# Attention and two matmuls on one core: twelve steps' leaky ReLU and the first batch's token sums in another form

## The chip, the core and the metric

The program runs on one core of a Trainium2 chip. The core has five engines with a queue of instructions each: PE (TensorE, matmuls; its weight loads are listed as PEld), DVE (VectorE), ACT (ScalarE), POOL (GpSimd) and SP, which here only issues DMAs. Each engine takes its instructions in order, and semaphores hold an instruction back until what it reads is written. SBUF is the working memory; PE writes to PSUM, in eight banks of 128x512 fp32.

The metric is the device time of one execution in microseconds. Before the change three runs took 1013.35 to 1014.5 us, with a median of 1014.16.

## The reference: what is computed

Two parts in a row, all in fp32.

Attention, for 8 batches, 8 heads, 576 tokens of 64 values:

```python
q_d = q.reshape(B, H, Sd, 4, D).mean(axis=3)          # the same for k, v
out_d = softmax(q_d k_d^T / 8) v_d
out_up = np.repeat(out_d, 4, axis=2)
mask = np.abs(pos[:, None] - pos[None, :]) < 4
out_local = softmax(where(mask, q k^T / 8, -1e9)) v
x = (out_up + out_local) as 4608 tokens x 512
```

So each token attends to its neighbours at a distance below four, and the means of four tokens attend to one another ("down").

Then two matmuls with a leaky ReLU between them, whose slope alpha belongs to the column:

```python
h = x @ w_in                                           # 4608x512 by 512x2048
g = np.maximum(h, 0.0) + alpha * np.minimum(h, 0.0)
out = g @ w_out                                        # 4608x2048 by 2048x512
```

The inputs w_in and w_out come as 64-bit floats and are put into fp32 on the chip by integer operations on their halves ("decode").

## The kernel before

**The two matmuls, in steps.** The 4608 tokens make 18 chunks of 256, and the 2048 columns of w_in 8 blocks of 256, so there are 144 steps; step s works on chunk s // 8 and block s % 8. Every operand is split into a rounded high part and a low part, and three products are summed. In a step, hidden(s) (L743) writes h into a PSUM bank of the pair ph with 24 matmuls; slopes(s) (L756) reads it on ACT, for each half once with the scale slope into an SBUF tile t and once with the scale sign back into the same bank; larger(s) (L763) takes the maximum of the two on DVE; split(s) (L766) casts it to the high part gh on ACT and subtracts on POOL for the low part gl; product(s) (L786) adds 12 matmuls to the output banks. sign is +1 where alpha is at most 1 and -1 elsewhere, slope is sign times alpha, and w_out's rows carry sign, so the maximum is right for both.

**The order of the steps** is written out by hand. Every part enters a list with a due time, at(t, f, ...), counted in steps, and the list is worked off in order of these times (L915 to L917). hidden(s) stands at s - 1.95, slopes at s - 1.45, larger at s - 1.15, split at s - 1.0 and product at s + 0.6. So PE works in the order hidden(s), product(s-2), hidden(s+1), product(s-1), hidden(s+2), product(s).

**The attention of batches 1 to 7** stands in the same list: local (L566) for the neighbours, on DVE mostly, and down (L224) for the means, whose loads ld are folded four to one by POOL's adds (L72), turned and scored by PE (qkT L250, s L263, pT L287, pv L297) and copied between by ACT (kd L258, dp L273 and L282, th L291, od L302).

**The first batch** has its own code (L363 to L522) ahead of the list, and there the framework's scheduler sets the order on each engine, by its own estimate of times. Four pairs of heads pass through pair(hp): q and k are turned by PE into the banks f0T, f1T and copied by ACT to qb and kT; the windows' scores fs get a maximum fmx, a difference fp, an exponential, a sum fsm and a normalization (L481 to L488) on DVE and ACT; PE turns fp into fpT and weighs v into fpv; DVE adds the down part fod into fxs, and ACT and DVE split it into xh and xl (L512 to L519), the first chunks' operands. The sums of four tokens of q and k are taken from the loaded tiles by two adds each on DVE (L453, L455) and turned by PE (L460); those of v by two adds (L471, L473). The pairs' down part waits for them.

**The decode** of a block of weights (make, L161) runs magnitude on ACT (L184), reach (L188, L189) and bits (L193, L194) on DVE, upper on ACT (L199 for w_in, L203 for w_out) and lower on DVE (L207, L211). The ten blocks with fp below 5 run with the first batch, 128x1024 at a time with the temporary in SBUF; the last twelve half blocks stand in the list, 128x512 at a time with the temporary in PSUM. In the page's and the trace's names, woh and wol are the high and low part of w_out, wih and wil those of w_in.

## Time and profile before

| | |
|---|---|
| median of three runs | 1014.16 us |
| the profiled execution | 1012.62 us, its span 1010.8 us |
| PE busy | 960.6 us (95%), 6402 instructions |
| DVE busy | 832.8 us (82%), 1347 |
| ACT busy | 560.2 us (55%), 1483 |
| POOL busy | 482.1 us (48%), 612 |
| mean DMA rate | 97 GB/s over the span |

The page divides the span into 40 slices of 25.3 us and gives busy shares in tenths. PE is at 9 from the eighth slice on, DVE at 8 or 9 in nearly all slices but the last four, and the DMA engines at 8 and 9 in the first two. TensorE's granted clock is below 9 in four of the first five slices. A row of the groups gives a line, an engine, the operation, what it writes and reads, the shape, a count, the busy time and the mean in ns of one, and the engine's idle time just before. The view of waits gives the waiting instruction, the one that released it, the total, the count and the longest. Windows give busy times for stretches of the span.

### The profile page before, as it was taken

The page shows a single profiled execution, that of the slowest core. Times are in us where ns is not written, and L with a number is a line of the kernel's source. Part 1 is how long each engine was busy: PE and PEld are TensorE (multiplying, and loading weights), DVE is VectorE, ACT ScalarE, POOL GpSimd, SP SyncE. Part 2 cuts the span into 40 slices and gives each one's busy share as a digit, 9 for nine tenths or more (in the row PEclk, how much of TensorE's full clock was granted, in tenths as well). Part 3 has the DMA queues.
Part 4 walks back from the last instruction along what each step waited for, and adds up shares of the span by engine and source line. Part 5 has one row for each costly group of instructions (what it writes and reads, how often), then busy time and mean ns, then how long its engine had stood idle before and what let it go on. Part 6 is the DMA issues. An engine that isn't in the chain of part 4 may idle for free.

```text
span 1010.8 us, 17864 instructions
## 1 busy us (share of the span) xinstructions
PE 960.6 (95%) x6402; PEld 852.7 (84%) x6402; DVE 832.8 (82%) x1347; ACT 560.2 (55%) x1483; POOL 482.1 (48%) x612
## 2 busy tenths in 40 slices
PE   5877989999999999999999999999999999999998
PEld 4756878898888898988888888888988898989997
DVE  6899988899888899899888898898898899997111
ACT  4767766465565555555455555555555554444442
POOL 2040645677665546555554544656555543323221
PEclk9856989999999999999999999999999999999999
DMA  8946443232422322433322332322331412210000
GB/s 191 222 148 242 123 153 98 83 119 83 145 83 73 118 81 78 121 97 93 103 88 66 100 111 71 125 80 74 123 100 60 131 49 61 86 43 22 1 21 22
DMA packets 61218, 98.26 MB, mean 97 GB/s; under 512 B 21578, under 2 KB 26954, under 8 KB 61130
## 3 DMA queue, kind: packets, MB, share of 16 engines
q1 hardware_dynamic: 60938, 96.87, 32.0%
q8 instruction: 50, 0.82, 0.3%
q10 hardware_dynamic: 192, 0.26, 0.1%
q14 instruction: 38, 0.31, 0.1%
HBM read 87.67 MB, written 9.44 MB: 96 GB/s over the span
## 4 chain that ended last, share of the span: by engine, by line
PE 72%; DVE 15%; ACT 4%; issue 3%; DMA 2%; POOL 2%; SPq 2%; DVEq 0%; ACTq 0%; POOLq 0%
PE o L798 33%; PE h L752 33%; DMA raw<-in_moe_w_out 2%; DVE qk L591 2%; DVE lb L650 2%; PE s L263 2%; DVE t L764 1%; PE pv L297 1%; DVE ls L595 1%; DVE temp L193 1%; DVE pv L647 1%; PE xp L659 1%; PE pT L287 1%; DVE temp L194 1%; DMA ld<-in_q 1%
## 5 line engine op out<-in xcount | busy, mean ns | idle before, releaser
L69 POOL TENSOR_TENSOR gl<-t,gh 128x512 fp32r<-128x512 f32 x144 | 186.5, 1295 | 390.8 <-ACT gh L769 347.4
L760 ACT ACTIVATE t<-h,slope 128x256 f32<-128x256 f32 x288 | 136.3, 473 | 203.0 <-PE h L752 166.2
L764 DVE TENSOR_TENSOR t<-h,t 128x512 f32<-128x512 f32 x144 | 99.0, 687 | 113.2 <-ACT h L761 108.6
L752 PE MATMUL h<-xh,wih 128*128 128x256 f32 x1152 | 190.9, 287 | 0.7 <-ACT xh L518 0.7
L798 PE MATMUL o<-woh,gh 128*128 128x512 f32 x576 | 188.1, 407 | 0.4 <-ACT woh L203 0.4
L752 PE MATMUL h<-xl,wih 128*128 128x256 f32 x1152 | 183.7, 281 | 0.6 <-POOL xl L69 0.6
L752 PE MATMUL h<-xh,wil 128*128 128x256 f32 x1152 | 184.1, 282 | 0.0
L798 PE MATMUL o<-wol,gh 128*128 128x512 f32 x576 | 182.1, 397 | 0.1
L798 PE MATMUL o<-woh,gl 128*128 128x512 f32 x576 | 182.1, 397 | 0.0
L752 PEld LDWEIGHTS h<-xh,wih 128*128 128x128 f32 x1152 | 163.5, 190 | 10.5 <-issue 1.8
L72 POOL TENSOR_TENSOR ld<-ld 72x256 f32<-72x256 f32 x168 | 125.4, 747 | 73.9 <-DMA ld<-in_q 49.4
L752 PEld LDWEIGHTS h<-xl,wih 128*128 128x128 f32 x1152 | 156.9, 190 | 0.8 <-POOL xl L69 0.8
L752 PEld LDWEIGHTS h<-xh,wil 128*128 128x128 f32 x1152 | 157.3, 190 | 0.0
L769 ACT CAST gh<-t 128x512 fp32r<-128x512 f32 x144 | 89.1, 619 | 118.7 <-DVE t L764 68.4
L595 DVE TENSOR_REDUCE ls<-qk 128x12 f32<-128x768 f32 (+1 forms) x126 | 136.4, 1083 | 2.8
L798 PEld LDWEIGHTS o<-woh,gl 128*128 128x128 f32 x576 | 108.6, 189 | 26.4
L798 PEld LDWEIGHTS o<-wol,gh 128*128 128x128 f32 x576 | 108.4, 188 | 26.4 <-DVE wol L211 0.7
L761 ACT ACTIVATE h<-h,sign 128x256 f32<-128x256 f32 x288 | 126.4, 439 | 0.0
L650 DVE TENSOR_TENSOR lb<-lb,pv 128x384 f32<-128x384 f32 x202 | 113.9, 564 | 5.5
L798 PEld LDWEIGHTS o<-woh,gh 128*128 128x128 f32 x576 | 98.3, 189 | 16.3 <-issue 2.2
L647 DVE TENSOR_TENSOR pv<-v,lb 128x1152 f32<-128x1152 f32 x84 | 93.6, 1115 | 2.6
L591 DVE TENSOR_TENSOR qk<-k,qp 128x768 f32<-128x768 f32 (+1 forms) x78 | 84.0, 1077 | 0.0
(148 smaller groups left out, 1111.4 us busy)
## 6 DMA issues: line engine op xcount, KB each, us to landing
k<-in_k SPq DMA_DIRECT2D x41, 384.0 KB
v<-in_v SPq DMA_DIRECT2D x41, 384.0 KB
raw<-in_moe_w_in SPq DMA_DIRECT2D x16, 512.0 KB
raw<-in_moe_w_out SPq DMA_DIRECT2D x16, 512.0 KB
ld<-in_q SPq DMA_DIRECT2D x56, 144.0 KB
ld<-in_k SPq DMA_DIRECT2D x56, 144.0 KB
ld<-in_v SPq DMA_DIRECT2D x56, 144.0 KB
q<-in_q SPq DMA_DIRECT2D x42, 192.0 KB
```

The source lines that it names most:

```text
L69: nc.gpsimd.tensor_tensor(o, a, b, op=ALU.subtract)
L72: nc.gpsimd.tensor_tensor(o, a, b, op=ALU.add)
L591: nc.vector.tensor_tensor(st["pr"][:, :nd], window(tiles[u, "k"], half, d0, nd), st["qp", half].unsqueeze(1).to_broadcast([128, nd, 2, 192 ...
L595: nc.vector.tensor_reduce(out=st["s"][:, half, d0:d0 + nd, :].rearrange("p a b -> p (a b)"), in_=st["pr"][:, :nd].rearrange("p a h (t d) - ...
L647: nc.vector.tensor_tensor(st["pr"][:, :nd], window4(tiles[u, "v"], half, d0, nd), prob(half, d0, nd), op=ALU.mult)
L650: nc.vector.tensor_tensor(st["acc"], st["acc"], st["pr"][:, i], op=ALU.add)
L752: nc.tensor.matmul(ph[:, j], w[:, m, 128 * o:128 * o + 128], x[:, m, :], start=(i == 0), stop=(i == 11))
L760: nc.scalar.activation(t[:, j], hs[st][:, j], AF.Copy, scale=slope[:, f:f + 1])
L761: nc.scalar.activation(hs[st][:, j], hs[st][:, j], AF.Copy, scale=sign[:, f:f + 1])
L764: nc.vector.tensor_tensor(gs[st], hs.pop(st), gs[st], op=ALU.max)
L769: nc.scalar.copy(gh, t)
L798: nc.tensor.matmul(outs[c][m], g[:, j, 128 * m:128 * m + 128], wo[w][n][:, o, :], start=(f == 0 and i == 0), stop=(f == NF - 1 and i == 2))
```

## The change

It has three parts.

1. In steps 0 to 11 (EARLY = 12) the second activation of slopes no longer writes sign times h into the PSUM bank: it writes Relu(gain times h), with gain = sign - slope, into an SBUF tile of the pool late with the tag xf, which has one buffer; larger then adds the two on POOL, where before it took the maximum on DVE. The ph bank is free once ACT has read it. Steps 12 to 143 are as they were.
2. For the first batch's q and k, the sums of four tokens are reduced on DVE from the PSUM banks f0T and f1T after PE has turned the tokens. The adds ahead of the turn, the four transposes of the sums and the copy of k's sums are gone.
3. The first batch's two adds for v move from DVE to POOL.

```diff
+EARLY = 12
+    gain = const.tile([128, NF], F32, name="gain")
...
+        nc.vector.tensor_tensor(gain, sign, slope, op=ALU.subtract)
...
         def pair(hp):
+            sums = [st.tile([128, 144], F32, tag=f"fs{x}", name=f"fs{x}{hp}") for x in "qk"]
             for x in range(2):
                 for t0, nt in ((0, 4), (4, 4)):
...
+                    nc.vector.tensor_reduce(out=sums[x][:, 18 * t0:18 * t0 + 72], in_=ps.rearrange("p (t a) -> p a t", t=nt),
+                                            axis=AX.X, op=ALU.add)
...
-                    sums = []
-                    for i, x in enumerate("qk"):
-                        lv = qk[hp][:, i].rearrange("p (g f) h d -> p g (f h d)", g=2)
-                        s4 = lv[:, :, 0:256]
-                        nc.vector.tensor_tensor(s4, lv[:, :, 0:256], lv[:, :, 256:512], op=ALU.add)
-                        s2 = st.tile([72, 2, 128], F32, tag=f"fs2{x}", name=f"fs2{x}{hp}")
-                        nc.vector.tensor_tensor(s2, s4[:, :, 0:128], s4[:, :, 128:256], op=ALU.add)
-                        sums.append(s2)
-                    ps = ps_h.tile([128, 512], F32, tag="ph", name=f"fsum{hp}")
-                    for x in range(2):
-                        for g in range(2):
-                            nc.tensor.transpose(ps[:, (2 * x + g) * 72:(2 * x + g) * 72 + 72], sums[x][:, g],
-                                                ident[:72, :72])
...
-                    kd = st.tile([128, 144], F32, tag="fkh", name=f"fkd{hp}")
-                    nc.scalar.copy(kd, ps[:, 144:288])
...
-                        nc.tensor.matmul(sd[:, bl, :], qd[:, bl, :], kd, start=True, stop=True)
+                        nc.tensor.matmul(sd[:, bl, :], qd[:, bl, :], sums[1], start=True, stop=True)
...
-            nc.vector.tensor_tensor(lv[:, :, 0:128], lv[:, :, 0:128], lv[:, :, 128:256], op=ALU.add)
+            add(lv[:, :, 0:128], lv[:, :, 0:128], lv[:, :, 128:256])
...
-            nc.vector.tensor_tensor(vd.rearrange("p h g d -> p (h g) d"), lv[:, :, 0:64], lv[:, :, 64:128], op=ALU.add)
+            add(vd.rearrange("p h g d -> p (h g) d"), lv[:, :, 0:64], lv[:, :, 64:128])
...
     def slopes(st):
         t = gs[st] = two.tile([128, 2, T], F32, tag="t", name=f"t{st}")
+        other = hs[st]
+        if st < EARLY:
+            other = late.tile([128, 512], F32, tag="xf", name=f"sh{st}").rearrange("p (j n) -> p j n", j=2)
         for j in range(2):
             f = 2 * (st % NP) + j
             nc.scalar.activation(t[:, j], hs[st][:, j], AF.Copy, scale=slope[:, f:f + 1])
-            nc.scalar.activation(hs[st][:, j], hs[st][:, j], AF.Copy, scale=sign[:, f:f + 1])
+            if st < EARLY:
+                nc.scalar.activation(other[:, j], hs[st][:, j], AF.Relu, scale=gain[:, f:f + 1])
+            else:
+                nc.scalar.activation(other[:, j], hs[st][:, j], AF.Copy, scale=sign[:, f:f + 1])
+        if st < EARLY:
+            hs[st] = other

     def larger(st):
-        nc.vector.tensor_tensor(gs[st], hs.pop(st), gs[st], op=ALU.max)
+        if st < EARLY:
+            add(gs[st], hs.pop(st), gs[st])
+        else:
+            nc.vector.tensor_tensor(gs[st], hs.pop(st), gs[st], op=ALU.max)
```

Since the scheduler orders the first batch anew, more moves than the diff shows. In the rows below, a number after a name's first word tells the pair (fmx2, fp2), the half and block of weights (raw0_1 is w_in's block 1, raw1_3 w_out's block 3) or the step (t0, gl0); the last number only tells buffers apart.

DVE, around the start of the decode of w_out's block 1 (raw1_1, whose first DVE instruction is the tensor_scalar L188 behind raw0_1's last L194). Before:

```order
L482 TENSOR_TENSOR fp2_576<-fs20_532,fmx2_573 128x490
L189 TENSOR_SCALAR temp_791<-temp_791 128x1024
L453 TENSOR_TENSOR fqk3_157<-fqk3_157 72x2x256
L482 TENSOR_TENSOR fp2_576<-fs27_541,fmx2_573 128x140
L519 TENSOR_TENSOR xl1_328<-fxs04_325,xh1_327 128x256
L193 SCALAR_TENSOR_TENSOR temp_791<-raw0_1_167,temp_791 128x1024
L455 TENSOR_TENSOR fs2q3_679<-fqk3_157 72x256
L453 TENSOR_TENSOR fqk3_157<-fqk3_157 72x2x256
L194 SCALAR_TENSOR_TENSOR temp_791<-raw0_1_167,temp_791 128x1024
L188 TENSOR_SCALAR temp_791<-temp_791 128x1024
```

With the change (L188 is L191 there, L194 is L197, L481, L482 and L488 are L472, L473 and L479):

```order
L197 SCALAR_TENSOR_TENSOR temp_765<-raw0_1_169,temp_765 128x1024
L440 TENSOR_REDUCE fsk2_476<-f1T20_493 128x72
L477 TENSOR_SCALAR fsm1_410<-fsm1_410 128x9
L191 TENSOR_SCALAR temp_765<-temp_765 128x1024
L440 TENSOR_REDUCE fsk2_476<-f1T24_500 128x72
L478 RECIPROCAL frs1_411<-fsm1_410 128x9
L192 TENSOR_SCALAR temp_765<-temp_765 128x1024
L210 TENSOR_TENSOR wil0_82<-temp_765,wih0_81 128x4x256
L479 TENSOR_TENSOR fp1_412<-fp1_412,frs1_411 128x630
L196 SCALAR_TENSOR_TENSOR temp_765<-raw1_1_175,temp_765 128x1024
L472 TENSOR_REDUCE fmx2_554<-fs20_513 128x7
L472 TENSOR_REDUCE fmx2_554<-fs27_522 128x2
```

Pair 2's difference fp2 (and its maximum fmx2 before it) stood ahead of that tensor_scalar and now stands behind it, as does pair 1's normalization (fp1), which stood earlier still.

DVE, around the last pair's first fxs (pair 3). Before:

```order
L194 SCALAR_TENSOR_TENSOR temp_791<-raw0_3_847,temp_791 128x1024
L188 TENSOR_SCALAR temp_791<-temp_791 128x1024
L189 TENSOR_SCALAR temp_791<-temp_791 128x1024
L207 TENSOR_TENSOR wil1_830<-temp_791,wih1_829 128x4x256
L512 TENSOR_TENSOR fxs30_770<-fpv30_761,fod3_759 128x256
L193 SCALAR_TENSOR_TENSOR temp_791<-raw1_3_857,temp_791 128x1024
L512 TENSOR_TENSOR rest_89<-fpv38_787,fod3_759 128x64
L188 TENSOR_SCALAR temp_791<-temp_791 128x1024
L519 TENSOR_TENSOR xl0_313<-fxs30_770,xh0_312 128x256
```

With the change (L512 is L503, L519 is L510):

```order
L210 TENSOR_TENSOR wil1_804<-temp_765,wih1_803 128x4x256
L510 TENSOR_TENSOR xl1_323<-fxs24_612,xh1_322 128x256
L196 SCALAR_TENSOR_TENSOR temp_765<-raw1_3_831,temp_765 128x1024
L191 TENSOR_SCALAR temp_765<-temp_765 128x1024
L197 SCALAR_TENSOR_TENSOR temp_765<-raw1_3_831,temp_765 128x1024
L192 TENSOR_SCALAR temp_765<-temp_765 128x1024
L503 TENSOR_TENSOR fxs30_744<-fpv30_735,fod3_733 128x256
L196 SCALAR_TENSOR_TENSOR temp_765<-raw0_4_843,temp_765 128x1024
L214 SCALAR_TENSOR_TENSOR wol1_816<-temp_765,sign_78,woh1_815 128x512 x2
L503 TENSOR_TENSOR rest_91<-fpv38_761,fod3_733 128x64
L510 TENSOR_TENSOR xl0_308<-fxs30_744,xh0_307 128x256
```

The two bit operations of raw1_3 stood behind the last pair's fxs and now stand ahead of it, with two tensor_scalars that now belong to raw0_4.

ACT, between the first step's activations and kd of the first down part. Before:

```order
L184 ACTIVATE temp_791<-raw1_4_881 128x1024
L199 CAST wih2_877<-temp_791 128x4x256
L769 CAST gh0_1007<-t0_995 128x512
L255 ACTIVATE qd32_84<-qkT1_0_1001 64x3x48 x2
L258 COPY kd1_0_1038<-qkT1_0_1001 128x144
```

With the change (L203 is L206, L769 is L771, L255 is L258, L258 is L261):

```order
L756 ACTIVATE sh0_970<-h0_944,gain_80 128x256
L206 ACTIVATE woh2_863<-temp_765,sign_78 128x512 x2
L771 CAST gh0_982<-t0_969 128x512
L258 ACTIVATE qd32_85<-qkT1_0_976 64x3x48 x2
L261 COPY kd1_0_1013<-qkT1_0_976 128x144
```

The cast of w_in's block 4 stood just ahead of gh0, qd and kd; now the two halves of w_out's block 4 stand there. On POOL each step's add t now stands directly ahead of gl of the same step, between the folds of ld.

More of the change, by code (lines that the diff above doesn't have):

```diff
@@ L448, in pair @@
                 else:
-                    sums = []
-                    for i, x in enumerate("qk"):
-                        lv = qk[hp][:, i].rearrange("p (g f) h d -> p g (f h d)", g=2)
-                        s4 = lv[:, :, 0:256]
-                        nc.vector.tensor_tensor(s4, lv[:, :, 0:256], lv[:, :, 256:512], op=ALU.add)
-                        s2 = st.tile([72, 2, 128], F32, tag=f"fs2{x}", name=f"fs2{x}{hp}")
-                        nc.vector.tensor_tensor(s2, s4[:, :, 0:128], s4[:, :, 128:256], op=ALU.add)
-                        sums.append(s2)
-                    ps = ps_h.tile([128, 512], F32, tag="ph", name=f"fsum{hp}")
-                    for x in range(2):
-                        for g in range(2):
-                            nc.tensor.transpose(ps[:, (2 * x + g) * 72:(2 * x + g) * 72 + 72], sums[x][:, g],
-                                                ident[:72, :72])
                     for e, r in enumerate(halves):
                         nc.scalar.mul(qd[r, :, 48 * e:48 * e + 48].rearrange("p b (i g) -> p b i g", g=2),
-                                      ps[r, 0:144].rearrange("p (g b i) -> p b i g", g=2, b=3), DSCALE)
-                    kd = st.tile([128, 144], F32, tag="fkh", name=f"fkd{hp}")
-                    nc.scalar.copy(kd, ps[:, 144:288])
+                                      sums[0][r].rearrange("p (g b i) -> p b i g", g=2, b=3), DSCALE)
                     sd = bank("d", f"fsd{hp}")[:96, 0:432].rearrange("p (b c) -> p b c", b=3)
                     for bl in range(3):
-                        nc.tensor.matmul(sd[:, bl, :], qd[:, bl, :], kd, start=True, stop=True)
+                        nc.tensor.matmul(sd[:, bl, :], qd[:, bl, :], sums[1], start=True, stop=True)
             lv = vt[hp].rearrange("p h (g f) d -> p (h g) (f d)", g=2)
-            nc.vector.tensor_tensor(lv[:, :, 0:128], lv[:, :, 0:128], lv[:, :, 128:256], op=ALU.add)
+            add(lv[:, :, 0:128], lv[:, :, 0:128], lv[:, :, 128:256])
             vd = st.tile([72, 2, 2, 64], F32, tag="fs2v", name=f"fvd{hp}")
-            nc.vector.tensor_tensor(vd.rearrange("p h g d -> p (h g) d"), lv[:, :, 0:64], lv[:, :, 64:128], op=ALU.add)
+            add(vd.rearrange("p h g d -> p (h g) d"), lv[:, :, 0:64], lv[:, :, 64:128])
             if EM[hp] == "b":
```

## The prediction

> **What bounds it now.** I read the windows by stage first (columns: stretch; length; busy time of PE, weight load, DVE, ACT, POOL; granted clock of TensorE; DMA share), with borders at the landing of the second w_out block, the last pair's first sum, the first product and the end of step 7.
>
> ```profile
> span 1010.8 us, 17864 instructions
> ```
>
> ```profile
> 41.40:49.74 8.34, 7.41 (x70) 5.85 (x69) 7.75 (x16) 7.40 (x19) 0.84 (x1) 0.70 0.99 255
> 49.74:83.62 33.88, 23.71 (x161) 18.19 (x161) 33.56 (x55) 22.95 (x56) 12.45 (x12) 0.50 0.47 160
> 83.62:99.85 16.23, 12.97 (x83) 12.58 (x84) 16.09 (x22) 10.83 (x25) 1.78 (x1) 0.75 0.73 256
> 99.85:156.90 57.05, 51.96 (x314) 43.60 (x313) 47.43 (x75) 39.62 (x100) 29.86 (x42) 0.94 0.42 131
> 156.90:200.00 43.10, 40.38 (x279) 35.73 (x278) 38.11 (x58) 24.07 (x66) 26.17 (x34) 1.00 0.34 104
> 200.00:1010.80 810.80, 796.15 (x5312) 711.83 (x5310) 659.52 (x1063) 432.85 (x1163) 405.31 (x498) 1.00 0.27 82
> ```
>
> Up to 49.74 the DMA engines are full (0.99). From 49.74 to 99.85 DVE is (33.56 of 33.88 us, 16.09 of 16.23). From 156.9 on PE is (796.15 of 810.8). Between 99.85 and 156.9 neither is: PE lacks 57.05 - 51.96 = 5.1 us, and runs at a mean clock of 0.94, which costs another 57.05 x 0.06 = 3.4 us: 8.5 us that shorter waits could give back. The chain of waits says why a gain before 49.74 is worth nothing:
>
> ```profile
> 37.77 10.70 DMA raw<-in_moe_w_out
> ```
>
> It is the second block of w_out, in flight until 48.47. What PE waits for between 85 and 200 us is in the view of waits:
>
> ```profile
> PE s L263 <- ACT kd L258: 3.4, 2, 2.1
> PE xp L659 <- ACT kd L258: 1.7, 1, 1.7
> PE qkT L250 <- ACT th L291: 1.7, 1, 1.7
> PE pT L287 <- ACT dp L282: 1.5, 1, 1.5
> PE qkT L250 <- POOL gl L69: 1.0, 1, 1.0
> ```
>
> The five longest. All but the last end on ACT's copies of small operands (kd, th, dp) for batch 1's down-sampled attention, and ACT's copies stand in its queue behind casts of weights that wait for DVE's decode. From step 12 the kernel is PE's; the change can only move the point from which PE runs without a gap.
>
> **The sums of the first batch.** Removed from DVE per pair: two adds of 72x512 (L453), two of 72x256 (L455), and for v one of each (L471, L473); from PE four transposes; from ACT the copy of kd.
>
> ```profile
> L453 DVE TENSOR_TENSOR fqk<-fqk 72x512 f32<-72x512 f32 x8 | 5.5, 682 | 0.4 <-PE f1T L425 0.2 <-PE f0T L425 0.2
> ...
> L471 DVE TENSOR_TENSOR fv<-fv 72x512 f32<-72x512 f32 x4 | 2.7, 683 | 4.6 <-DMA fv<-in_v 4.6
> ...
> L488 DVE TENSOR_TENSOR fp<-fp,frs 128x630 f32<-128x630 f32 x2 | 1.6, 804 | 0.0
> ```
>
> Added per pair: four reductions 128x72 out of 288 elements of PSUM on DVE, and two adds on POOL. All eight L453 and all four L471 lie before 49.74, under the DMA, so their removal is worth nothing. What counts is the stretch from 49.74 to the last pair's fxs, where DVE is full. Its groups (count; busy us, mean ns; idle before):
>
> ```profile
> L194 DVE SCALAR_TENSOR_TENSOR temp<-raw,temp 128x1024 int32<-128x1024 int32 x4 | 4.9, 1223 | 0.0
> L193 DVE SCALAR_TENSOR_TENSOR temp<-raw,temp 128x1024 int32<-128x1024 int32 x4 | 4.9, 1213 | 0.0
> L188 DVE TENSOR_SCALAR temp<-temp 128x1024 f32<-128x1024 f32 x5 | 3.8, 757 | 0.6 <-ACT temp L184 0.6
> L207 DVE TENSOR_TENSOR wil<-temp,wih 128x1024 fp32r<-128x1024 f32 x3 | 3.6, 1194 | 0.0
> L189 DVE TENSOR_SCALAR temp<-temp 128x1024 int32<-128x1024 int32 x5 | 3.4, 676 | 0.0
> L211 DVE SCALAR_TENSOR_TENSOR wol<-temp,sign,woh 128x512 fp32r<-128x512 f32 x4 | 2.8, 742 | 0.0
> L519 DVE TENSOR_TENSOR xl<-fxs,xh 128x256 fp32r<-128x256 f32 x4 | 2.1, 538 | 0.0
> L488 DVE TENSOR_TENSOR fp<-fp,frs 128x630 f32<-128x630 f32 x2 | 2.1, 1066 | 0.0
> L512 DVE TENSOR_TENSOR fxs<-fpv,fod 128x256 f32<-128x256 f32 x5 | 2.0, 410 | 0.0
> ...
> L473 DVE TENSOR_TENSOR fvd<-fv 72x256 f32<-72x256 f32 x2 | 1.1, 526 | 0.0
> L455 DVE TENSOR_TENSOR fs2k<-fqk 72x256 f32<-72x256 f32 x1 | 0.9, 940 | 0.0
> L482 DVE TENSOR_TENSOR fp<-fs,fmx 128x490 f32<-128x490 f32 x1 | 0.7, 651 | 0.0
> L481 DVE TENSOR_REDUCE fmx<-fs 128x7 f32<-128x490 f32 x1 | 0.6, 647 | 0.0
> ...
> L481 DVE TENSOR_REDUCE fmx<-fs 128x2 f32<-128x140 f32 x1 | 0.3, 291 | 0.0
> L482 DVE TENSOR_TENSOR fp<-fs,fmx 128x140 f32<-128x140 f32 x1 | 0.3, 285 | 0.0
> ```
>
> All groups of this view sum to 37.7 us and fill 33.56, since ends overlap: an instruction is worth 0.89 of its mean. The order has moved: with the load of that w_out block as landmark, pair 1's normalization (L488, 1.07) and pair 2's maxima and differences (0.65 + 0.65 + 0.29 + 0.29) stood ahead of its L188 and now stand behind it; and ahead of the last pair's fxs now stand four more decode instructions (L193 1.21, L194 1.22, L188 0.76, L189 0.68). Five reductions fall into the stretch, one L455 (0.94) and two L473 (0.53 each) leave it. A reduction of 288 elements is not in the trace; L481 takes 0.291 us for 140 and 0.647 for 490 elements, so it lies between these, and in proportion at 0.44, which I take. Sum: 1.07 + 1.88 + 3.87 + 5 x 0.44 - 2.0 = 7.0, times 0.89 = 6.2 us. So the last pair's fxs comes 6.2 us later, at about 89.8, but with 3.4 us of decode already done that used to follow. Bounds: the reductions by L481's two rows, 0.8 either way; L488 swells here to 1066 ns from 804, with POOL's adds running beside it, and a like share of L488, L519, L473 and L455 (a quarter of 6.2 us) may go or double, 1.5 either way: 3.9 to 8.5.
>
> POOL's v adds: nothing was ever there but the downs' adds; by the row of POOL below, 0.73 for 72x256 and 1.30 for 128x512, 2.0 us per pair, hidden where POOL idles (0.84 us busy in 41.40:49.74), unless they hold DVE (a rival).
>
> **From fxs to the first product.** Ahead of kd ACT now has woh of block 4, which needs that block's last L194, and from fxs to there DVE has 13 instructions: L512 0.41 x 2, L193 1.21 x 2, L194 1.22 x 2, L211 0.74 x 2, L519 0.54 x 2, L188, L189, L207: 10.9, times 0.89 = 9.7 us. Before, the matching rows are
>
> ```profile
> 91.02 1.22 DVE L194 SCALAR_TENSOR_TENSOR temp<-raw,temp 128x1024 int32<-128x1024 int32 x1
> ```
>
> ```profile
> 94.65 0.62 PE L263 MATMUL s<-kd,qd 128*96 128x144 f32 x3 [2.13 <-ACT kd L258]
> ```
>
> 94.65 - 92.24 = 2.4 us from L194 to PE's matmul through ACT. So 9.7 + 2.4 = 12.1 us after fxs against 94.65 - 83.62 = 11.0: 1.1 later. PE waits there either way. Bounds: 0 (woh finds its operand earlier) to 2.1 (the wait in the row above once more). The first product is then 6.2 + 1.1 = 7.3 us late.
>
> **The twelve sums.** Each takes a 128x512 max from DVE and puts a 128x512 add on POOL, and ACT's second activation writes SBUF:
>
> ```profile
> L764 DVE TENSOR_TENSOR t<-h,t 128x512 f32<-128x512 f32 x7 | 4.7, 678 | 0.0
> ```
>
> ```profile
> L72 POOL TENSOR_TENSOR ld<-ld 72x256 f32<-72x256 f32 x17 | 12.4, 731 | 5.6 <-DMA ld<-in_v 4.9 <-DMA ld<-in_q 0.8
> L69 POOL TENSOR_TENSOR gl<-t,gh 128x512 fp32r<-128x512 f32 x8 | 10.4, 1302 | 22.3 <-ACT gh L769 22.2
> ```
>
> ```profile
> L760 ACT ACTIVATE t<-h,slope 128x256 f32<-128x256 f32 x288 | 136.3, 473 | 203.0 <-PE h L752 166.2
> ...
> L761 ACT ACTIVATE h<-h,sign 128x256 f32<-128x256 f32 x288 | 126.4, 439 | 0.0
> ```
>
> The activation becomes one like L760: 473 instead of 439 ns, 24 x 0.034 = 0.8 us of ACT, which is busy 39.6 of 57 us, and counts as nothing; if ACT were full it would cost 0.8. A Relu is not in the trace; as an activation of the same shape I take L760, with L761's 439 as the lower end. The add: gl's 1.30 us, so 12 x 1.3 = 15.6 us more on POOL, which has 27 us idle in the stretch. It lengthens one step's chain by 1.30 - 0.68 = 0.6, but after hidden(s) PE has two products and two more hidden blocks before product(s), which hides it. Queued behind the add on POOL stand split's gl and the folds; what could hold the add is a fold that waits for its load (5.6 us idle in L72's row, once 4.9).
>
> DVE loses seven maxima between 99.85 and 156.9: 7 x 0.68 = 4.7 us, and the 3.4 us of decode were done ahead: by the last decode DVE has made up 8.1 of 7.3. The waits of PE for kd, dp and th then end where PE arrives, for PE is the late one by 7.3 us. I expect 6.8 of the 8.5 us back: what stays is the th copy, behind woh in ACT's queue, and the last w_out block, whose woh follows hidden(8) itself (0.9 and 0.8: half of the waits qkT <- th, 1.7, and pT <- dp, 1.5, as an estimate). After that, 43.1 - 40.38 = 2.7 us idle up to 200 (xp <- kd 1.7 and qkT 1.0), with three maxima more off DVE: I take 2.2. Of the 14.7 us without PE after 200 I take 0.6 (0 to 1.5), since only DVE's lead at 200 can shorten them.
>
> **Sum:** +6.2 + 1.1 - 6.8 - 2.2 - 0.6 = -2.3 us. The profiled execution took 1012.62 us (span 1010.8 and 1.8 around it) and lies 1.5 below the median of the runs, 1014.16; the same difference gives 1011.9. Ends: 3.9 + 0 - 8.5 - 2.7 - 1.5 = -8.8, and 8.5 + 2.1 - 4 - 0 - 0 = +6.6.
>
> **Rivals.** (1) All waits go: 3.4 us decode ahead and seven maxima less make ACT's queue run ahead of PE everywhere, and the stage before grows only by 5: 5 + 1.1 - 8.5 - 2.7 - 1.5 = -6.6, 1007.6. For it: every wait in the view is on ACT behind decode. Against: woh of the last block hangs on hidden(8).
> (2) Slower: the first product's 7.3 us are not given back. The place is the in-order queue of ACT: its copies kd, th, dp wait behind woh and gh, and gh now waits for POOL instead of DVE. If half of the 8.5 and a third of the 2.7 come back, 7.3 - 4.3 - 0.9 = +2.1; if POOL's add also stands behind a fold that waits for its load, 1.3 more: +3.4, 1017.6. It decides when less than 5.3 us of waits come back. For it: the waits name ACT or POOL, never DVE. Against: ACT's idle time ends on DVE's decode.
> (3) POOL and DVE hold each other up. Rows:
>
> ```profile
> 94.49 1.76 DVE L189 TENSOR_SCALAR temp<-temp 128x1024 int32<-128x1024 int32 x1
> ```
>
> ```profile
> 93.91 1.78 POOL L69 TENSOR_TENSOR gl<-t,gh 128x512 fp32r<-128x512 f32 x1 [31.63 <-ACT gh L769]
> ```
>
> L189 took 1.76 instead of 0.68 us while gl ran. Two adds of steps 0 and 1 and two late v sums of 0.73 now fall where decode works from SBUF to SBUF. If each holds DVE for its whole length, 2 x 1.3 + 2 x 0.73 = 4.1 us: -2.3 + 4.1 = +1.8, 1016.0, no change by the measure below; if the half, +0.2. [...]
> (4) The sums on POOL are no relief, since xf has one buffer and ACT's next second activation waits for the add: ACT then follows POOL. The next comes a step later (57.05 us for eight), so the add would have to be some 5 us late; the wait of a fold for its load (4.9, above) comes near it once. If that costs 2 us of PE, -2.3 + 2 = -0.3, 1013.9.
>
> **Chances.** What a measurement of this kernel can tell from no change is about 0.2%, 2.0 us. Forecast 0.48 (its own range 1008.5 to 1015): two thirds of it beyond 2.0, 0.32 faster, 0.16 same. Rival 1 0.16, faster. Rival 2 0.23, slower. Rival 3 0.07 and rival 4 0.06: 0.10 same, 0.03 slower. Faster 0.48, same 0.26, slower 0.26. The range takes the lower end nearly whole, since rival 1 lies there, and cuts the upper one just above rival 2: 1005.5 to 1018.0.
>
> **What would show it.** The last pair's fxs at 88 to 92 instead of 83.62, behind DVE still without idle time; if at 84 or before, the first term is wrong. The first product at about 107. Between there and the end of step 7 (about 157.4) PE with under 2 us idle and a clock near 1.0; if it still waits for kd, dp and th, rival 2. POOL's adds at 1.3 us after 100; decode rows of 1.7 us before it mean rival 3. Both activations of an early step at 0.47. If PE is not 1 to 3 us ahead of before's 156.9 at the end of step 7 or soon after, the sum is wrong, whatever the time.

## The result, and the profile after

The changed kernel took 1020.87 us (median of five runs, 1018.46 to 1021.39) against 1014.16 (1013.19 to 1014.5): a ratio of 1.0055, 95% interval 1.0042 to 1.0068. By that ratio it is slower by 5.6 us (the two medians lie 6.7 apart), where I had forecast 2.3 us less. Measured again (e9 below) it was 1.0038 (1.0021 to 1.0055), so 4 to 6 us.

The windows by stage of the changed kernel, with the borders of the prediction: VectorE's first instruction on the second w_out block (the prediction calls this border, 49.74 before, the landing, which by its own row is 1.3 us earlier), the last pair's first fxs, the first product, the end of step 7, the end of the wait at xp, the end (columns as before: stretch, length, PE, weight load, DVE, ACT, POOL, clock, DMA share, GB/s).

```profile
48.45:88.55 40.10, 32.46 (x228) 26.86 (x228) 40.10 (x67) 27.21 (x64) 11.45 (x14) 0.54 0.43 149
88.55:107.39 18.84, 14.20 (x84) 13.51 (x84) 13.43 (x21) 12.72 (x32) 6.15 (x4) 0.70 0.68 237
107.39:159.47 52.08, 48.68 (x314) 41.32 (x313) 40.90 (x64) 35.83 (x92) 37.24 (x48) 1.00 0.41 126
159.47:204.36 44.89, 40.36 (x279) 35.70 (x278) 36.52 (x55) 23.85 (x66) 29.90 (x37) 1.00 0.32 99
204.36:1016.60 812.24, 797.57 (x5312) 713.16 (x5311) 659.31 (x1063) 433.68 (x1163) 405.40 (x498) 1.00 0.26 82
```

Against before: the first product is 7.5 us later (107.39 against 99.85). The next stage takes 52.08 us instead of 57.05, so 5.0 come back. The stage up to the wait at xp takes 44.89 instead of 43.10: 1.8 more are lost. The rest takes 812.24 instead of 810.80: 1.4 more. 7.5 - 5.0 + 1.8 + 1.4 = 5.7, and the spans (1016.6 and 1010.8) differ by 5.8. The profiled execution took 1018.46 us; it is the fastest of the five.

What PE waits for, 85 to 205 us, five of the six longest:

```profile
PE s L266 <- ACT kd L261: 3.8, 1, 3.8
PE qkT L253 <- POOL gl L70: 2.8, 1, 2.8
PE qkT L253 <- ACT th L294: 2.6, 1, 2.6
PE xp L650 <- ACT kd L261: 1.7, 1, 1.7
...
PE pT L290 <- ACT dp L285: 0.4, 1, 0.4
```

The wait for kd at the first scores grew from 2.1 to 3.8, those of the transposes qkT from 1.0 and 1.7 to 2.8 and 2.6; pT <- dp shrank from 1.5 to 0.4, and the second kd wait (1.3 of the 3.4 before) is gone.

DVE, which had hardly any idle time between fxs and the first product before (16.09 of 16.23 us busy), is now busy for 13.43 of 18.84. Its waits from 88 to 108:

```profile
DVE dnb L270 <- PE s L266: 2.2, 1, 2.2
DVE drs L281 <- ACT dsm L278: 1.5, 1, 1.5
DVE temp L191 <- ACT temp L187: 0.9, 1, 0.9
DVE wol L214 <- ACT woh L206: 0.8, 1, 0.8
```

So the decode that was done ahead of fxs did not bring the next block forward; DVE had nothing to do. The stage after it starts like this, on POOL, ACT and DVE (start, length, in brackets the idle time before and what ended it):

```profile
109.07 0.73 POOL L73 TENSOR_TENSOR ld<-ld 72x256 f32<-72x256 f32 x1 [2.12 <-DMA ld<-in_q]
...
110.30 0.72 POOL L73 TENSOR_TENSOR ld<-ld 72x256 f32<-72x256 f32 x1
...
111.52 1.29 POOL L73 TENSOR_TENSOR t<-sh,t 128x512 f32<-128x512 f32 x1
```

```profile
112.84 0.62 ACT L771 CAST gh<-t 128x512 fp32r<-128x512 f32 x1 [3.16 <-POOL t L73]
113.37 0.58 ACT L202 CAST wih<-temp 128x512 fp32r<-128x512 f32 x1
```

```profile
113.98 0.69 DVE L210 TENSOR_TENSOR wil<-temp,wih 128x512 fp32r<-128x512 f32 x1 [2.84 <-ACT wih L202]
```

The sum of step 2 stands on POOL behind two folds, the first of which waited for its load until 109.07. gh(2) waited 3.16 us for the sum, and in ACT's queue behind gh(2) stands wih, the first cast of block 5; DVE waited 2.84 for that. The first wil of block 5 comes at 113.98; before the change it came at 107.10, without a wait:

```profile
107.10 0.68 DVE L207 TENSOR_TENSOR wil<-temp,wih 128x512 fp32r<-128x512 f32 x1
```

At step 8 the same queue costs PE 1.8 us more than before. POOL, ACT and PE:

```profile
160.37 0.46 POOL L73 TENSOR_TENSOR s2v<-ld 72x128 f32<-72x128 f32 x1
161.75 0.75 POOL L70 TENSOR_TENSOR xl<-rest,xh 128x256 fp32r<-128x256 f32 x1 [0.93 <-ACT xh L826]
162.46 1.27 POOL L73 TENSOR_TENSOR t<-sh,t 128x512 f32<-128x512 f32 x1
```

```profile
161.27 0.41 ACT L826 CAST xh<-rest 128x256 fp32r<-128x256 f32 x1
163.76 0.62 ACT L771 CAST gh<-t 128x512 fp32r<-128x512 f32 x1 [2.09 <-POOL t L73]
164.29 1.07 ACT L806 COPY sg<-o 128x512 f32<-128x512 f32 x2
165.24 0.70 ACT L294 COPY th<-pT 72x288 f32<-72x288 f32 x2
```

```profile
162.34 0.63 PE L743 MATMUL h<-xl,wih 128*128 128x256 f32 x4
165.79 0.32 PE L253 MATMUL qkT<-ident,s2q 72*128 72x72 f32 x2 [2.83 <-POOL gl L70]
```

place_rest's subtraction (xl) is ahead of the sum of step 9 on POOL and waits for ACT's xh; the sum ends at 163.73, gh(9) has held ACT for 2.09 us, and th, which frees the bank of qkT, comes behind gh(9) and the two sg. The view names gl as releaser, but by the times th is what came last. Before the change gh(9) did not wait:

```profile
159.36 0.62 ACT L769 CAST gh<-t 128x512 fp32r<-128x512 f32 x1
```

The last 1.4 us are TensorE's clock. The wait of pT for lb (2.5 us) is in both traces; after it the clock stays at 1.00 before and drops in the changed kernel. After, then before:

```profile
532.00:534.00 2.00, 0.24 (x2) 0.27 (x3) 1.86 (x8) 0.97 (x4) 1.54 (x2) 0.85 0.58 186
534.00:536.00 2.00, 2.00 (x12) 2.00 (x11) 1.86 (x5) 0.74 (x3) 1.92 (x4) 0.50 0.61 202
536.00:538.00 2.00, 2.00 (x16) 2.00 (x16) 0.62 (x1) 0.00 (x0) 1.19 (x3) 0.80 0.37 117
```

```profile
527.64:529.64 2.00, 0.32 (x4) 0.35 (x5) 1.86 (x8) 0.97 (x4) 1.63 (x2) 1.00 0.62 196
529.64:531.64 2.00, 2.00 (x20) 2.00 (x19) 1.86 (x5) 0.56 (x2) 1.92 (x4) 1.00 0.61 195
531.64:533.64 2.00, 2.00 (x14) 1.76 (x14) 0.53 (x1) 0.94 (x3) 1.19 (x3) 1.00 0.33 103
```

The loss of the three rows is 2 x (0.15 + 0.50 + 0.20) = 1.7 us, so 3.4 us at half clock.

### The profile page after: what moved, and what is told of

It is laid out like the page before. It is cut to its first block, busy times and chain, and to the rows that moved or that the text cites. A ratio compares the mean times of both kernels' runs of the same rounds, so it can differ in the third digit from the quotient of the medians.

```text
span 1016.6 us, 17809 instructions
## 1 busy us (share of the span) xinstructions
PE 961.8 (95%) x6386; PEld 854.7 (84%) x6386; DVE 822.4 (81%) x1328; ACT 560.3 (55%) x1479; POOL 503.7 (50%) x632
## 4 chain that ended last, share of the span: by engine, by line
PE 72%; DVE 14%; ACT 5%; POOL 2%; issue 2%; DMA 2%; SPq 2%; DVEq 0%; ACTq 0%; POOLq 0%
PE h L743 33%; PE o L800 33%; PE s L266 2%; DVE lb L641 2%; DMA raw<-in_moe_w_out 2%; DVE qk L582 2%; PE pv L300 1%; DVE ls L586 1%; DVE pv L638 1%; DVE t L766 1%; DVE temp L197 1%; PE pT L290 1%; PE xp L650 1%; DVE temp L196 1%; ACT t L754 1%
## 5 line engine op out<-in xcount | busy, mean ns | idle before, releaser
L766 DVE TENSOR_TENSOR t<-h,t 128x512 f32<-128x512 f32 x132 | 90.9, 688 | 114.5 <-ACT h L758 107.1
L743 PEld LDWEIGHTS h<-xh,wih 128*128 128x128 f32 x1152 | 163.7, 191 | 10.4 <-issue 2.0
L771 ACT CAST gh<-t 128x512 fp32r<-128x512 f32 x144 | 89.1, 619 | 121.4 <-DVE t L766 63.4
L758 ACT ACTIVATE h<-h,sign 128x256 f32<-128x256 f32 x264 | 116.0, 439 | 0.0
## 6 DMA issues: line engine op xcount, KB each, us to landing
q<-in_q SPq DMA_DIRECT2D x42, 192.0 KB
```

Source lines behind the costliest of these rows:

```text
L743: nc.tensor.matmul(ph[:, j], w[:, m, 128 * o:128 * o + 128], x[:, m, :], start=(i == 0), stop=(i == 11))
L758: nc.scalar.activation(other[:, j], hs[st][:, j], AF.Copy, scale=sign[:, f:f + 1])
L766: nc.vector.tensor_tensor(gs[st], hs.pop(st), gs[st], op=ALU.max)
L771: nc.scalar.copy(gh, t)
```

## The experiments

**Theory A:** the time was lost in order, not in work. The first batch's new order delays the first product; decode and sums are tied to the steps by ACT's in-order queue, so DVE's relief cannot make it up, and at two places PE waits behind ACT's queue whatever DVE does. **Theory B:** the sums on POOL are what loses. **The prediction's view:** DVE's amount of work sets the end of the decode.

All were timed in five rounds beside the kernel before, whose runs on these chips spread over 1010.8 to 1021.4 us; the ratios below go by those. A single trace is therefore read by its stages, and this table (us, from the traces: the last pair's first fxs; the start of product 0; from product 5 to 6; from product 7 to 8; the start of product 13; from there to the end) is what the experiments are judged by.

| kernel | ratio (95%) | fxs | product 0 | 5 to 6 | 7 to 8 | product 13 | rest |
|---|---|---|---|---|---|---|---|
| before | 1 | 83.6 | 99.9 | 12.4 | 8.5 | 196.2 | 814.6 |
| changed | 1.0055 (42 to 68) | 88.5 | 107.4 | 11.1 | 9.9 | 200.6 | 816.1 |
| e9, changed again | 1.0038 (21 to 55) | 88.0 | 107.2 | 13.7 | 9.6 | 203.5 | 816.3 |
| e1, sums only | 1.0013 (-4 to 29) | 82.3 | 100.0 | 13.8 | 9.6 | 198.8 | 816.2 |
| e2, first batch only | 1.0022 (5 to 39) | 90.0 | 104.5 | 13.7 | 8.5 | 202.4 | 814.6 |
| e13, q and k only | 1.0019 (5 to 32) | 89.0 | 103.1 | 13.4 | 8.5 | 199.7 | 814.7 |
| e4, v only | 1.0054 (33 to 75) | 84.8 | 101.8 | 13.8 | 8.5 | 200.8 | 818.2 |
| e5, remainder later | 1.0020 (6 to 34) | 88.0 | 105.9 | 12.3 | 8.2 | 199.8 | 814.6 |
| e7, four behind fxs | 1.0058 (35 to 80) | 86.9 | 104.7 | 13.6 | 9.6 | 203.3 | 816.3 |
| e12, decode early | 1.0014 (-4 to 33) | 89.4 | 107.3 | 9.4 | 8.3 | 199.4 | 818.2 |
| e10, remainder, th | 1.0024 (6 to 41) | 85.6 | 101.9 | 10.5 | 8.5 | 195.8 | 816.7 |
| e14, all three | 0.9981 (-31 to -6) | 88.5 | 106.3 | 8.3 | 7.8 | 195.1 | 816.6 |
| e6, before, no maxima | 0.9980 (-34 to -7) | 83.6 | 97.7 | 13.4 | 8.5 | 195.2 | 814.7 |
| e8, before, th first | 0.9973 (-43 to -11) | 84.4 | 100.6 | 10.4 | 8.7 | 195.2 | 816.2 |
| e16, the same again | 0.9958 (-54 to -30) | 82.8 | 99.1 | 10.8 | 8.5 | 194.0 | 816.1 |
| e15, th, decode early | 0.9941 (-74 to -44) | 82.3 | 97.4 | 7.8 | 8.4 | 191.0 | 814.6 |
| e18, the same again | 0.9957 (-59 to -27) | 86.6 | 101.7 | 7.6 | 8.4 | 195.4 | 814.6 |
| e11, sums, remainder, th | 0.9982 (-38 to +1) | 87.3 | 103.4 | 10.5 | 8.5 | 197.9 | 816.6 |
| e17, sums and all orders | 0.9977 (-40 to -5) | 81.5 | 99.2 | 9.7 | 8.0 | 192.0 | 818.3 |

(The interval is given in ten-thousandths above or below 1.)

**e1 and e2: the two halves.** e1 has the first batch of before, e2 is the changed kernel with

```diff
-EARLY = 12
+EARLY = 0
```

> The twelve step sums on GpSimd alone; the first batch as in the kernel before. Theory A (the time was lost in the first batch's new order, and the step sums only fail to give it back): the last pair's first fxs at 83.6 as before, the first product within 1 us of 99.85, the end of step 7 between 154.5 and 157, then up to 2.8 us lost at the product of step 8, whose th copy waits behind a gh that waits for the sum; in all -2.5 to +1.5 us, 1011.5 to 1015.5. Theory B (the step sums are what loses, since gh and with it ACT's copies wait for GpSimd's 1.3 us instead of VectorE's 0.68): slower by 3 to 5 us, 1017 to 1019, with the end of step 7 at 158 or later.

> The first batch's part alone (reductions for q and k, GpSimd for v); every step's maximum on VectorE as before. Theory A: fxs at 88.5, the first product 4 to 6 us later than before (103.9 to 105.9; the casts of block 4's woh stand behind kd here, so without the 2.6 us that the changed kernel lost between fxs and the product), the end of step 7 at 158 to 160; in all +2 to +5 us, 1016 to 1019. Theory B: all of it but 1 us is given back by the end of step 7, 1013 to 1015.

e1's waits of PE:

```profile
PE s L266 <- ACT kd L261: 2.9, 1, 2.9
PE qkT L253 <- POOL gl L70: 2.8, 1, 2.8
PE qkT L253 <- ACT th L294: 2.6, 1, 2.6
```

Theory A at both places: e1 reaches the first product as before (100.0) and product 7 at the same time (153.1 in both traces, seven maxima off DVE notwithstanding), then loses at step 8 with the same 2.8 us as the changed kernel; e2 starts 4.6 late and is 6.2 late at product 13. In e2 the casts of block 4's woh stand behind kd on ACT, in the changed kernel ahead of it: e2's first product is 2.9 us earlier than the changed kernel's, though its fxs is 1.5 later.

> The changed kernel once more, on the chip and beside the runs of the kernel before that the other experiments have, since these scatter more here (1011 to 1020 us) than in its first measurement (1013.2 to 1014.5). Expected 4 to 7 us over the kernel before, as then; were it 0 to 2.5, the parts measured alone (sums 1.3, first batch 2.2) would simply add up and nothing would be left for an interaction.

e9 lost 3.9 us (2.1 to 5.6), the two halves 1.3 and 2.2, 3.5 together. Both have their share, and the intervals are too wide to show an interaction.

**e3, e13 and e4: the parts of the first batch.** e4 is the kernel before with v's four adds as add(...), e13 the changed kernel with EARLY = 0 and v's adds as nc.vector.tensor_tensor. e3 was meant as e13, but my edit also moved the first adds of the later batches' folds to DVE.

> Only the reductions for q and k; v's sums stay on VectorE, the steps as before. If the reductions in the full stretch are the loss: fxs at 87 to 90, the first product 4 to 7 us late, 1016 to 1019. [...] A reduction of 288 elements takes 0.45 us either way.

> The reductions for q and k alone: v's sums on VectorE in the first batch, every fold of the later batches on GpSimd and every maximum on VectorE as in the kernel before. If the reductions' place in VectorE's order delays the start as the whole first-batch part does: fxs at 87 to 91, first product at 103 to 107, 1016 to 1019. If v's sums were what delayed it: fxs at 83 to 85.5, and 1013 to 1015.5. If any new order of the first batch delays it by some us (v alone did, by 2.0 at the first product), the reductions too lie between: first product 101 to 103.

> Only v's sums on GpSimd; the rest as before. VectorE loses two instructions of 0.53 us in its full stretch and six that lie under the DMA. If v's sums are harmless: fxs 0 to 2 us earlier than 83.6, 1012 to 1014.5. If GpSimd holds VectorE up where both run (two sums of 0.73 beside the decode): rows of 1.7 us where 0.68 is usual, fxs 1 to 3 us later, 1015 to 1017.

e3 took 1.0684 (1.0657 to 1.0711) and tells nothing of the first batch, only that 168 folds of 0.63 us (105.8 us) on DVE cost 69 us. In e13 fxs comes at 89.0 and the first product at 103.1, so in this trace the edit to q and k alone brings nearly all of the delay that the whole part has in e2. Whether it is the reductions (0.45 us each) or the new order that any edit brings there is not shown: 103.1 is at the border of those two forecasts. e4 only takes work off DVE and costs 5.4 us. The scheduler laid the first batch out anew there too: pair 1's sum and normalization now stand ahead of pair 2's token sums, which came first before. Its trace has no more decode rows held up beside POOL than the one before (one of 1.64 against one of 1.76), so rows held up by v's sums on POOL are not the cause. How much of the 5.4 us is the start, one trace cannot tell, for the start itself varies: in the nine traces with the order of the kernel before, fxs comes between 81.5 and 87.3 (median 83.6), in the seven with the changed kernel's, between 85.6 and 90.0 (median 88.5). The 4.9 between the medians are what the new order did; e4's cause stays open.

**e7: four decode instructions behind fxs.**

```diff
...
-                    for f in make(which, fp):
-                        f()
+                    for i, f in enumerate(make(which, fp)):
+                        if (fp, which, i) >= (3, 1, 2):
+                            with tc.issue_after(summed[3, 0].ins):
+                                f()
+                        else:
+                            f()
```

summed[3, 0] is the last pair's first fxs; the edges set issue order only.

> The changed kernel with the decode of block 3 of w_out from its bits on, and that of block 4, queued behind the last pair's first fxs on VectorE; nothing is added or removed. If four instructions ahead of fxs are 3.4 of its delay (the prediction's first term): fxs at 85 to 86 instead of 88.55, and since the casts of block 4's woh then stand behind kd, the first product at 100.5 to 103 instead of 107.4; the decode is then 3.4 us further behind, and product 7 comes at 153.5 to 156. In all 1.5 to 3 us better than the changed kernel. If the reductions themselves are the delay: fxs at 87.5 or later and no gain.

fxs came 1.6 us earlier and the first product 2.7, less than expected and within the scatter of the start. Product 13 was at 203.3, as in e9, and the time is the changed kernel's (1.0058); the last decode instruction came at 158.8, in e9 at 159.0. Whether the four stand ahead of fxs or behind it makes no difference that these runs can tell.

**e6: what is DVE's relief worth by itself?**

```diff
-        nc.vector.tensor_tensor(gs[st], hs.pop(st), gs[st], op=ALU.max)
+        h = hs.pop(st)
+        if st >= 8:
+            nc.vector.tensor_tensor(gs[st], h, gs[st], op=ALU.max)
```

The maxima of steps 0 to 7 are left out, with nothing in their place.

> The kernel before with the maxima of the first eight steps left out (so its output is not the reference's): VectorE is relieved of 8 x 0.68 = 5.4 us, and GpSimd gets nothing. If VectorE's decode bounds steps 0 to 7 (what the prediction's third term rests on): product 7 starts at 146.5 to 149.5 instead of 153.1, and the whole takes 4 to 7 us less. If ACT and PE's own steps pace the decode of w_out (casts that stand behind the activations of a step), and only the w_in blocks are bound by VectorE: product 7 at 151 to 153, the last decode instruction at 152 to 154.5 instead of 155.1, the whole 0 to 2.5 us less.

2.0 us (0.7 to 3.4) for 5.4 us of DVE: the lower forecast. Product 7 at 152.1, last decode instruction at 154.0. DVE's waits of 100 to 160 us, in the kernel before and here:

```profile
DVE wol L211 <- ACT woh L203: 5.8, 4, 2.6
DVE temp L188 <- ACT temp L184: 2.6, 3, 1.3
```

```profile
DVE wol L211 <- ACT woh L203: 7.3, 4, 3.5
DVE temp L188 <- ACT temp L184: 3.3, 4, 1.6
```

A part of what is taken off DVE (2.2 of 5.4 us) reappears as waits for ACT's casts, 8.4 before and 10.6 here.

**e12: the decode's lead.**

```diff
-T0_DEC, D_DEC = 0.5, 0.56
+T0_DEC, D_DEC = 0.1, 0.56
...
-    decoded = t
+    decoded = t + 0.4
```

> The changed kernel with the decode of blocks 5 to 7 due 0.4 of a step earlier (remainder and loads of u 3 left where they were). In the changed kernel VectorE is ahead at the first product and idles 5.4 us there. If that lead is lost because the next block's first cast stands on ACT behind the activations of steps 1 and 2: the first wil of block 5 at 109 to 112 instead of 114.0, the last decode instruction at 153.5 to 156 instead of 157.6, product 7 0.5 to 2 us earlier than 156.2, the time 0.5 to 2 us below the changed kernel. If VectorE's amount of work sets it (as the prediction summed it): the first wil no earlier than 113 and the same time within 0.6 us.

The first casts of block 5 now stand ahead of gh(2) on ACT:

```profile
110.03 0.69 DVE L210 TENSOR_TENSOR wil<-temp,wih 128x512 fp32r<-128x512 f32 x1 [1.68 <-ACT wih L202]
```

Block 5's first wil at 110.03 instead of 113.98, the last decode instruction at 153.1 instead of 157.6, product 7 at 155.1 instead of 156.2; the ratio is 1.0014 beside e9's 1.0038 on the same chip, 2.4 us. The two intervals overlap, but the twelve runs of each have means of 1016.0 and 1019.5. That is theory A: the lead was there and ACT's order kept it from use.

**e5, e8 and e10: the two places where PE waits behind ACT.** e5 changes the changed kernel, e8 the kernel before, e10 has both in the changed kernel:

```diff
-    at(decoded + 0.6, place_rest)
+    at(decoded + 0.64, place_rest)
```

```diff
-FIRST = (-1.3, 0.3, 3.0, 5.7)
+FIRST = (-1.3, 0.28, 3.0, 5.7)
```

The first takes place_rest from 7.82, just ahead of larger(9) at 7.85, to 7.86, behind it. The second breaks a tie: th of batch 1's second pair and slopes(7) were both due at 5.55, and slopes(7) was entered first.

> The changed kernel with the remainder's operands (place_rest) due 0.04 of a step later, so that they stand behind the sum of step 9 on GpSimd instead of ahead of it, and nothing else. If the loss at steps 8 and 9 is that sum standing behind the remainder's subtraction (gh(9) then holds ACT, and the th copy behind it PE): the wait of the transposes at step 8 falls from 2.8 to about 1.0 us as in the kernel before, the offset of product 13 against before falls from 4.4 to about 2.5 us, the time by about 1.8 us. If the wait is for the sum on GpSimd as such (1.3 us instead of 0.68): 0 to 0.6 us.

> The kernel before with the down-sampled attention of batch 1's second pair due 0.02 of a step earlier, so that its two th copies stand ahead of step 7's four activations on ACT instead of behind them. If that order alone makes the wait of the transposes at step 6 (1.7 us before, 2.6 after, whatever VectorE has to do): the wait falls below 0.6 us and product 6 starts 1 to 1.7 us earlier; the whole is 0.8 to 1.7 us faster. If the decode of w_out holds PE there anyway: the wait moves to the product, 0 to 0.5 us.

> The changed kernel with both small changes of order: the remainder behind the sum of step 9, and the second pair's th copies ahead of step 7's activations. If the two losses are separate places: the transposes at step 6 wait under 0.6 us (2.6 in the changed kernel), those at step 8 about 1.0 to 1.4 (2.8), product 9 at 168 to 170 instead of 173.2, and a time of 1012.5 to 1015.5, level with the kernel before. If the end of the decode (157.6 in the changed kernel) holds PE instead: product 8 still at 165 and 1016 to 1018.

e5's and then e8's waits of PE:

```profile
PE s L266 <- ACT kd L261: 3.1, 2, 2.9
PE qkT L253 <- ACT th L294: 2.6, 1, 2.6
PE xp L650 <- ACT kd L261: 1.7, 1, 1.7
PE qkT L253 <- POOL gl L70: 1.4, 1, 1.4
```

```profile
PE s L263 <- ACT kd L258: 4.3, 3, 2.2
...
PE xp L659 <- ACT kd L258: 1.7, 1, 1.7
PE pT L287 <- ACT dp L282: 1.5, 1, 1.5
PE qkT L250 <- POOL gl L69: 1.0, 1, 1.0
```

e5: the wait at step 8 falls from 2.8 to 1.4, from product 7 to 8 takes 8.2 instead of 9.9, and the ratio is 1.0020, 1.8 us below e9's, as forecast, though on another chip and with intervals that overlap. e8: qkT no longer waits for th at step 6, product 6 follows product 5 in 10.4 instead of 12.4, and the kernel before becomes faster by 2.7 us (1.1 to 4.4), and 4.3 when measured again (e16, where 1.1 us of the wait are left). That is more than the wait of 1.7, and in e16 a part of it is the clock: the kernel before has two stretches at half clock between 136 and 147 us (3.4 us lost), e16 has a clock of 0.93 from 136 to 140 and of 0.64 from 140 to 144, so 4 x (0.07 + 0.36) = 1.7 us lost. e10's trace has product 9 at 168.5, as expected, with an unusually early start (fxs at 85.6); its runs stayed at 1.0024, 1.4 us better than e9 and above the forecast.

**e14, e15, e16 and e18: the whole loss?** e14 is the changed kernel with the edits of e5, e8 and e12; e15 the kernel before with e8's, T0_DEC = 0.3 and decoded = t + 0.2; e16 and e18 repeat e8 and e15.

> The changed kernel with the remainder behind the sum of step 9, the second pair's th copies ahead of step 7's activations, and the decode of blocks 5 to 7 due 0.4 of a step earlier. If the three places are the whole loss: the first product still 5 to 7 us late, but product 9 within 1.5 us of 168.8 and product 13 within 1.5 us of 196.2, the ratio to the kernel before 0.997 to 1.001. If the late first product cannot be made up: product 9 at 170.5 or later, ratio 1.002 or more.

> The kernel before with th ahead of step 7's activations and the decode of blocks 5 to 7 due 0.2 of a step earlier. VectorE has no idle time before the first product there, so if VectorE's amount of work sets the decode: nothing beyond the th order alone (ratio 0.996 to 0.998). If ACT's order sets it in this kernel too: 0.994 to 0.996.

e14: the first product is still 6.5 us late (106.3), but product 13 is at 195.1 and the ratio is 0.9981. So against the kernel before, the three edits undo the loss. But they are not only a repair: e15, the kernel before with two of them, is the version that beats both kernels, at 1009.75 us, 0.9941 (0.9926 to 0.9956), and 0.9957 when repeated. It reached the faster of its two forecasts, so ACT's order sets the decode there as well. Nearly like for like (e14 against e15, on one chip; e14 has the decode 0.4 of a step earlier and e15 0.2) the change still costs 4 us, at product 13 too (195.1 against 191.0), with a first product that is 8.9 later.

**e11 and e17: are the sums worth anything?** e1 with the edits of e5 and e8, then with T0_DEC = 0.3 too.

> The sums of twelve steps on GpSimd with the first batch of the kernel before, and both small changes of order. If the sums cost nothing once they do not stand behind the remainder, and the th order is worth what it was in the kernel before (2.7 us): 1010.5 to 1013. If the sums are a gain of their own there: below 1010.5. If gh waits for GpSimd cost in other places: 1013.5 or more.

> The kernel before with the twelve step sums on GpSimd, the remainder behind the sum of step 9, th ahead of step 7's activations and the decode of blocks 5 to 7 due 0.2 of a step earlier. If VectorE's relief (twelve maxima) is worth something once nothing else holds the decode: 2 to 4 us below e18, 0.990 to 0.992. If it is worth nothing, since ACT and PE's steps pace the decode: within 1 us of e18. If the sum's longer chain (1.3 us against 0.68, and gh waiting for GpSimd) costs: 1 to 4 us above e18.

e11 is at 0.9982, the first of its forecasts. e17 is at 0.9977 beside 0.9957 of e18 on its chip, the last of its three: with these orders the sums on POOL bring nothing and cost about 2 us (means of twelve runs 1012.5 and 1010.3, though the intervals of the ratios overlap). So a small part of theory B stays; its place was not found.

## Why the prediction was wrong

The forecast summed +7.3 (the first two terms), -6.8, -2.2 and -0.6; the traces show +7.5, -5.0, +1.8 and +1.4. So the start came as summed, and the three terms that were to give it back failed, by 1.8, 4.0 and 2.0 us.

**The first term was right.** The last pair's fxs came at 88.55 (88 to 92 forecast, 89.8 by the sum), and DVE was busy for the whole 40.10 us before it. Its stretch grew from 33.88 to 40.10, the 6.2 us of the sum, and began 1.3 earlier. A reduction takes 0.45 us where I took 0.44. A fit this close is luck, since the start scatters by several us (e4 above), and its pieces were not shown one by one: the four decode instructions, put behind fxs again, gave 1.6 us (e7) where the sum had 3.4.

**The second was right in sum, not in parts.** First product at 107.39, forecast 107. But the piece after fxs was 2.6 us longer, not 1.1: 1.7 of it lie ahead of the scores, whose kd stood behind woh and gh(0) (101.24 - 88.55 = 12.7 us after fxs, 12.1 by the sum), and 0.9 behind them, where 5.5 us passed at half clock (3.4 before): the clock is 0.50 from 99.89 to 106.71, and from 95.13 to 98.54 before.

**The third failed: "by the last decode DVE has made up 8.1 of 7.3", hence 6.8 us back.** 5.0 came back, 3.4 of them the clock, which stayed at 1.00 this time (in e9, the same code, product 5 to 6 took 13.7 us instead of 11.1). In the page before, the clock is below 9 in the second, third, fourth and sixth slice, and these 3.4 us lie in the sixth (126 to 152 us), with 0.50 from 136.09 to 139.50 and from 142.91 to 146.32. The 3.4 us of decode done ahead became 5.4 us of idle DVE, because the next block's casts stand on ACT behind steps 1 and 2 (e12). The decode from the first wil of block 5 on did get shorter, from 48.0 us (107.1 to 155.1) to 43.6 (114.0 to 157.6), and to 46.0 in e9, with its longer 13.7 us; but it began 6.9 later, and with an on-time start the maxima are worth 2.0 (e6), because the blocks of w_out wait for ACT's casts between the steps, as the waits of e6 show. I had read "DVE is full" from stages and put one price on all its work; the waits it has itself (wol <- woh, 5.8 us) were in the trace and I did not ask for them. Of the waits that stay I had counted 0.9 for th; it was 2.6, and 2.6 or 2.7 in nine of the eleven traces in which slopes(7) stands ahead of th.

**The fourth failed: "three maxima more off DVE: I take 2.2".** 1.8 more were lost: the sum of step 9 queued behind place_rest on POOL (e5, e1), and the wait xp <- kd, most of which I had expected to go, stayed at 1.7. I had written of the queues "split's gl and the folds" and left out place_rest's subtraction, due 0.03 of a step earlier.

**The fifth** (0.6 back after 200): nothing came back, for the part from product 13 on takes 814.6 us before and in e2 and e5 alike, and 814.6 or 814.7 in e13, e15 and e18; before and in these three the clock is 1.00 in every window of 4 us from 204 to 996 us. The 1.4 us lost are a clock drop of 1.7 that kernels with and without the change have (below).

**The rivals.** Rival 2 is what happened: its place (ACT's in-order queue, with gh now waiting for POOL), its condition (less than 5.3 come back) and its extra (a sum behind a fold that waits for its load, once at step 2). Its price, 2.1 to 3.4, was too low by the step 9 place and the clock. I gave it 0.23 since "ACT's idle time ends on DVE's decode"; that is true, but the decode in turn waits for ACT. Rival 1 did not come: PE's longest waits for kd and th grew (3.8 and 2.6), and the relief of DVE by itself was worth 2.0 us (e6). Of rival 3 a little is to be seen: from 48.45 to 88.55, where POOL's folds ran beside them, five L196 took a mean of 1332 ns (1213 before) and three L210 1385 (1194), 1.2 us in all. But the stretch before had such rows too (L455 0.94 instead of 0.41, L519 0.95 instead of 0.41, L188 0.94 instead of 0.68, L488 1.33 instead of 0.80), so this is no loss of the change. (Half of rival 3's price gives -2.3 + 2.05 = -0.2, not the +0.2 of the prediction.) On POOL the first sum took longer:

```profile
97.31 1.22 DVE L197 SCALAR_TENSOR_TENSOR temp<-raw,temp 128x1024 int32<-128x1024 int32 x1
```

```profile
97.57 2.08 POOL L73 TENSOR_TENSOR t<-sh,t 128x512 f32<-128x512 f32 x1 [25.95 <-ACT sh L756]
```

2.08 us, where the sum of step 2 above took 1.29, while DVE's 1.22 is as ever (the mean of L197 from 48.45 to 88.55 is 1208 ns). The two overlap, and DVE's began 0.26 us before; what made the sum longer is not shown. Rival 4 (the single buffer of xf) shows nowhere: no activation waits for a sum in the view of waits.

## What to carry to other kernels

Before work is taken off a full engine, ask for that engine's own waits in the stage that counts: if it waits for casts of another in-order engine there, the saving becomes idle time, and the order of that other queue is where the time is (0.02 of a step at one tie was worth 2.7 us here, and no work changed). An operation moved to another queue must be checked against everything due just ahead of it there, also what has nothing to do with it. An edit inside a region that a list scheduler orders has to be priced by the new order; here the work on DVE in the full stretch changed by 0.2 us (five reductions came, one L455 and two L473 went), and the start moved by 5 to 7.

## What I had not expected of the hardware

In these traces TensorE's clock is at 0.50 for stretches of one length or a multiple of it, and the same wait does not always bring one. In the traces before and after the change such a stretch lasts 3.41 us or a multiple (6.83, 30.72, 34.13 and 40.96), except the one that the end of the span cuts off, and the borders of a trace's stretches lie whole multiples of 3.41 us apart.

From product 13 to the end the same instructions take 814.6 to 814.7 us in seven of the table's 19 traces, 816.1 to 816.7 in nine and 818.2 to 818.3 in three. A stretch costs 1.7 us there, 3.4 at half clock. Up to 996 us the windows have none in the kernel before, e13, e15 and e18 (814.6 to 814.7), one in the changed kernel, e14 and e16 (816.1 to 816.6) and two in e17 (818.3). The one in the changed kernel follows the 2.5 us wait for lb. Those of e14, e16 and e17 from 528 us on follow 4 us with PE busy for 2.12, 1.49 and 1.48; e18, with 2.12 from 524 to 528 too, has none. In the changed kernel the wait lies in the 3.41 us from 529.97 to 533.38, where PE was busy for 0.38, and the next 3.41 are at 0.50. Before, the same wait of 2.5 us lies across a border: PE was busy for 0.48 from 525.20 to 528.62 and for 0.79 from there to 532.03, and the clock stayed at 1.00. A share at which the clock drops is not shown: in the kernel before, the 3.41 us from 132.67 (0.58) and from 139.50 (0.50) were followed by a drop, those from 190.70 (0.50) were not.

So the wait for lb cost itself and, in the changed kernel, 1.7 us more; 12 of the 19 traces are longer by 1.4 us or more in that part. This and the start, which moves by 4 to 6 us between traces with the same order there, are the two sources of spread that the traces show.
